# Six sums of weights moved from block 1 to behind batch 0's rows, and a multiplication by g moved from block 2's second group to its third

## The chip, the cores and the metric

The kernel runs on one core of a Trainium2 chip. The metric is the time of one execution in device microseconds (us), as the median of several runs. A profiled execution gives the trace: its span is the time from the first to the last instruction, and its own time has a little more around it. The engines are TensorE (PE), VectorE (DVE), ScalarE (ACT), GpSimd (POOL) and SyncE (SP), each with a queue of its own that it works through in order. PEld is TensorE's load of weights, beside its products.

## The reference

Eight batches of eight heads, 576 tokens, 64 values a head. Attention without a softmax, a normalization with a gain g, and then a gated layer with GELU and a gated residual:

```python
kv = np.einsum('bhsd,bhse->bhde', k, v)
out = np.einsum('bhsd,bhde->bhse', q, kv)
rms = np.sqrt(np.mean(out * out, axis=-1, keepdims=True) + 1e-06)
x = out / rms * g_norm          # then (4608, 512), heads side by side
g = x @ w_gate                  # (4608, 1536)
gelu = 0.5 * g * (1.0 + erf(g * inv_sqrt2))
ffn_out = gelu * (x @ w_val) @ w_out
res_gate = 1.0 / (1.0 + np.exp(-(x @ w_res)))
result = x + res_gate * ffn_out
```

## The kernel before

The rows are worked in nine blocks. Blocks 0 to 7 hold the first 512 tokens of each batch, as four groups of 128 rows (`NJ = 4`); block 8 holds what remains of all eight batches. While a block is in the gated layer, the attention of a later batch is computed in between.

A block's first half multiplies its transposed rows, `xT_t[blk]`, by the weights of the gate and of the value, 12 tiles of 128 columns (`NF = 12`). Block 1 takes the tiles one by one (`m_gval`, lines 434 for TensorE, 422 for ScalarE's GELU, 423 for VectorE's product `hid`). From block 2 on, the columns come in three groups of four tiles (`gv_group`). A group computes its 2 by 2 blocks of products with seven products instead of eight, with sums of weights and sums of rows made beforehand. The weight sums are `wsg` and `wsv` (`weight_sums`, one `tensor_tensor` of VectorE at line 503 for each part; all of the kernel's `sub` calls have this line). The token sums are `ts` (`token_sums`). One set of weight sums is made for each group and each of gate and value: four sums a set. For group 0, whose columns lie in two tiles of weights, each sum takes two instructions of 128x256. Block 0 uses the seven products for its last group alone, so the sums of group 0 are wanted first by block 2.

The order of words within a group is a string, `ORDERS`. A digit with g or v is a product on TensorE (four matmuls, line 971); E and d are ScalarE's copies; F and c are VectorE's sums (line 992); g11 to g22 are GELUs; h11 to h22 are the products `hid` (line 1008; h22 on GpSimd, the others on VectorE). For the last group it is

```python
True: "1g 1v Eg 5g Ev 5v dg 6g dv 6v Fg 2g Fv 2v 7g g11 7v cg 3g cv 3v h11 g22 4g g12 h12 4v g21 h22 h21",
```

Product 7 adds to the bank that F has read, so 7g waits for Fg, and 7v for Fv.

The second half of a block (`out_by_products`, lines 540 and 503) multiplies `hid` by the output weights, again with seven products: wA, wD, wE and wF are TensorE's banks. Its last product, on wA, waits for VectorE's subtraction `osb` at line 503, which reads the bank first. Block 0 does this half plainly, with 48 matmuls (`out_by_f`, fps at line 472).

Attention of a batch b: `a_qT` or a transposing transfer gives qT, `a_kv` the 64x64 products, `a_o` the outputs `op`; ScalarE squares them (`a_sq`, line 263), VectorE reduces the squares (`a_red`, line 268, `ss`), `a_norm` makes the inverse root (on VectorE for batches 1 and 2, on GpSimd later), `a_t` writes the rows t (line 368), and a transpose, on TensorE for batch 1 (`a_xT`, xtp, line 375) and by a transfer later (`d_xT`), gives xT. The gain g enters xT by `a_g`, one `tensor_scalar` of VectorE at line 394 for two groups of rows; the rows t themselves, which the residual needs, are multiplied by g in `row_times_g` (line 385): for batch 0 on VectorE (`a_x`), for later blocks on GpSimd.

What sets the order: the program is written out by hand. Each block has numbered slots. `at(blk, slot, ...)` puts work behind a slot, `aside_out(blk, word, ...)` at a named point of the second half ("D", "F", "00", "22", "01", "11", "end"), and `at_word(blk, group, word, ...)` behind a word of a group. Each instruction goes to its engine's queue in the order in which the program reaches it. In block 0, slot 15 (`NF + 3`) is the point behind the fourth product of the residual gate; `plan_attn_1` puts batch 1's qT, the loads of batch 2 (GpSimd's queue) and batch 0's rows there. The reductions of batch 1 come next on VectorE, from `amid_step[3, 1]`. In block 1, slot 2 comes early in the gate and value products, slots 10 and 11 at their end.

`plan_attn_ahead(b)` spreads the attention of batch b over block m = b - 2 and the next. For b = 3, block m + 1 is block 2, the first that is `whole` (all three groups by seven products): `first_whole`.

Of the kernel before, what the change touches and what calls it, by code (L numbers as in the profile page):

```python
# [18 lines left out]
def kernel(  # L19
# [115 lines left out]
    def by_token(b, copy=nc.vector.tensor_copy, js=slice(0, NJ)):  # L135
        copy(
            out=b16_t[b, "q"].rearrange("p j h d -> p h j d")[:, :, js, :],
            in_=raw[b, "q"].rearrange("p h (j d) -> p h j d", j=NJ)[:, :, js, :],
        )
# [39 lines left out]
    def attn_begin(b):  # L179
        st[b] = {  # L180
            "qT": attnp.tile([P, NJ, NP, P], FP16, tag="qT", bufs=1, name="qT"),
            "kv2": (
                attnp.tile([P, NP, D], FP16, tag="kv2", bufs=4, name="kv2")
                if b > 0
                else t_t[B][:, NJ - 1, :].rearrange("p (r c) -> p r c", r=NP)
            ),
            "ss": attnp.tile([P, NJ + 1, H], FP32, tag="ss", name="ss"),
            "o": {},
        }

    def a_qT(b, jj):

        q16 = b16_t[b, "q"].rearrange("p j h d -> p j (h d)")
        ps = pattn.tile([P, 2, NP, P], FP16, tag="at", name="qtp")
        for e in range(2):
            for pr in range(NP):
                nc.tensor.transpose(ps[:, e, pr, :], q16[:, 2 * jj + e, pr * P : (pr + 1) * P], ident)
        nc.scalar.copy(out=st[b]["qT"][:, 2 * jj : 2 * jj + 2, :, :], in_=ps)
# [71 lines left out]
    def a_ss(b, i):  # L270
        a_sq(b, i)
        a_red(b, i)
# [81 lines left out]
    def where(b, j):  # L354
        return (b, j) if j < NJ else (B, pair(b))

    def a_t(b, i):

        o, rinv = st[b]["o"][i], st[b]["rinv"]
        if i < NJ:  # L360
            jj, e = i // 2, i % 2
            t = t_t[b][:, 2 * jj : 2 * jj + 2, :].rearrange("p j (r e d) -> p j r e d", e=2, d=D)[:, :, :, e, :]
            scale = of_o(rinv, i)[:, :, :, None].to_broadcast([P, 2, NP, D])
        else:
            t = t_t[B][:, pair(b), :].rearrange("p (h d) -> p h d", h=H)
            o = o.rearrange("p (h d) -> p h d", h=H)
            scale = rinv[:, NJ, :, None].to_broadcast([P, H, D])
        nc.vector.tensor_tensor(out=t, in0=o, in1=scale, op=ALU.mult)  # L368

    def a_xT(b, j, eng=nc.scalar):  # L370

        blk, jj = where(b, j)
        ps = pattn.tile([P, NP, P], FP16, tag="at", name="xtp")
        for cc in range(NP):
            nc.tensor.transpose(ps[:, cc, :], t_t[blk][:, jj, cc * P : (cc + 1) * P], ident)
        if eng is nc.scalar:
            nc.scalar.activation(out=xT_t[blk][:, jj, :, :], in_=ps, func=AF.Copy, scale=gcol)
        else:
            eng.tensor_scalar(out=xT_t[blk][:, jj, :, :], in0=ps, scalar1=gcol, scalar2=None, op0=ALU.mult)

    def a_x(b, j, eng=nc.vector):
        row_times_g(*where(b, j), eng)

    def row_times_g(blk, jj, eng):
        eng.tensor_tensor(out=t_t[blk][:, jj, :], in0=t_t[blk][:, jj, :], in1=g16, op=ALU.mult)  # L385

    def a_g(b, j0, j1, eng=nc.vector):

        blk, k0 = where(b, j0)
        xs = xT_t[blk][:, k0 : k0 + j1 - j0, :, :]  # L390
        if eng is nc.scalar:
            nc.scalar.activation(out=xs, in_=xs, func=AF.Copy, scale=gcol)
        else:
            eng.tensor_scalar(out=xs, in0=xs, scalar1=gcol, scalar2=None, op0=ALU.mult)
# [955 lines left out]
    def attn_plan_1():  # L1350

        b = 1
        ss = [lambda j=j: a_ss(b, j) for j in range(NJ)]
        t = [lambda j=j: a_t(b, j) for j in range(NJ)]
        x = [lambda j=j: a_xT(b, j) for j in range(NJ)]
        plan = {
            NF - 1: [lambda: by_token(b)],
            NF + 3: [
                lambda: attn_begin(b),
                lambda: a_qT(b, 0),  # L1360
                lambda: a_qT(b, 1),
                lambda: load_batch(b + 1),
                *[lambda j=j: a_x(0, j) for j in range(NJ)],
            ],
            NF + 6: [lambda: a_kv(b, nc.scalar.copy)],
            NF + 8: [lambda: a_norm(b, 0, NJ), *t],
            2 * NF + 2: [x[0]],
        }
        amid_step[3, 1] = [lambda: a_o(b), *ss]
        amid_step[NF - 1, 1] = [x[1], lambda: a_xT(b, 2, nc.vector)]  # L1370
        amid_step[NF - 1, 3] = [x[3]]
        return plan
# [13 lines left out]
    def at(blk, slot, *fs):  # L1386
        plans[blk].setdefault(slot, []).extend(fs)

    def aside_out(blk, ahead_of, *fs):
        amid_out.setdefault(blk, {}).setdefault(ahead_of, []).extend(fs)  # L1390
# [32 lines left out]
    def plan_attn_ahead(b):  # L1423

        rem = pair(b) is not None
        m = b - 2
        assert rem == (m in GROUPS)
        act, pool = nc.scalar.copy, nc.gpsimd
        begin = [lambda: attn_begin(b), lambda: d_qT(b)]
        if rem:  # L1430
            at_word(m, 0, "h22", begin.pop(0), lambda: d_rem_qT(b))
        if m in GROUPS:
            for i in range(2):
                half = lambda i=i: by_token(b, act, slice(2 * i, 2 * i + 2))
                if whole(m):
                    at_word(m, i, "g11", half)
                else:
                    at(m, 2 + i, half)
            if whole(m):
                at_word(m, 1, "g11", *begin)  # L1440
            else:
                at(m, 3, *begin)
            if b + 1 < B:
                at(m, 2 * GF, lambda: load_behind(b))
            last = len(GROUPS[m]) - 1
        else:
            at(m, 8, lambda: by_token(b, act, slice(0, 2)))
            at(m, 9, lambda: by_token(b, act, slice(2, 4)), *begin)
            at(m, NF, lambda: a_kv(b, act), lambda: load_behind(b, load_q))
            aside_out(m, "end", lambda: load_kv(b + 1))  # L1450
        if rem:
            at_word(m + 2, 0, "cv", lambda: a_g(b, NJ, NJ + 1))
            own = 2 * pair(b) + 1 == b
            at_word(m, last, "5v" if own else "3g", lambda: a_rem_kv(b))
            at_word(m, last, "dv" if own else "g12", lambda: kv_out(b))
            if own:
                at_word(m, last, "3g", lambda: rem_mm(b))
            at_word(m, last, "g12", lambda: rem_out(b))
        else:
            at(m, NF + 1, lambda: a_o(b), lambda: a_ss(b, 0), lambda: a_ss(b, 1))  # L1460
            aside_out(m, "D", lambda: a_ss(b, 2), lambda: a_ss(b, 3))
        aside_out(m, "F", lambda: a_norm(b, 0, NJ + rem, pool))
        first = [lambda: new_block(b), lambda: a_t(b, 0), lambda: a_t(b, 1)]
        if whole(m + 1):
            aside_out(m, "01" if m + 1 == WHOLE else "11", *first[0:2])
            upper = [] if m + 1 == WHOLE else [lambda: d_xT(b, 0, 2)]
            amid_out[m].setdefault("end", [])[0:0] = [first[2], *upper]
        else:
            at(m, NF + 3, *first)
        if whole(m + 1):  # L1470
            t = [lambda j=j: a_t(b, j) for j in range(NJ)]
            if rem:
                at_word(m + 1, 0, "h21", lambda: a_t(b, NJ), lambda: d_xT(b, NJ, NJ + 1))
            first_whole = m + 1 == WHOLE
            for i, word, fs in (
                (0, "Fv", t[2:3]),
                (0, "cv", [t[3], lambda: d_xT(b, 0 if first_whole else 2, NJ)]),
                (1, "h21" if first_whole else "cv", [lambda: a_g(b, 0, 2)]),
                (2, "Fv", [lambda: a_g(b, 2, NJ)]),
            ):  # L1480
                at_word(m + 1, i, word, *fs)
            return
        for j in range(2, NJ + rem):
            at(m + 1, j - 2, lambda j=j: a_t(b, j))
        at(m + 1, 1, lambda: d_xT(b, 0, NJ))
        at_word(m + 1, 1, "Fv", lambda: a_g(b, 0, 2))
        at_word(m + 1, 1, "cv", lambda: a_g(b, 2, NJ))
# [6 lines left out]
    at(0, 7, *sums["v", 2][0:2])  # L1494
    at_word(0, 0, "1v", *sums["v", 2][2:4])
    late_sums = [f for u in (("g", 0), ("v", 0)) for f in sums[u]]
    for i, f in enumerate(late_sums[0:6]):
        at(1, (2, 10, 11)[i // 2], f)
    aside_out(1, "22", *late_sums[6:8])
    for blk in GROUPS:  # L1500
        t = token_sums(blk, nc.vector)
        if blk == 2:
# [169 lines left out]
```

## Time and profile before

| | us |
|---|---|
| median of 3 runs (320.03 to 321.11) | 320.2 |
| profiled execution | 321.38 |
| its span | 319.6 |
| blocks 0 and 1's start: VectorE busy, 37.3 to 55.0 | 14.27 of 17.70 |
| block 1's first half: VectorE busy, 55.0 to 77.3 | 20.48 of 22.30 |
| block 1's second half: VectorE busy, 77.3 to 91.7 | 13.57 of 14.40 |
| block 2's three groups: VectorE busy, 91.7 to 112.0 | 19.25 of 20.30 |

The stages are windows of the trace, in us from the span's start. The mean granted clock of TensorE is 0.99. The page's slices of the span, in tenths of each fortieth, show how the engines are filled:

```profile
PE   7899999999999999999999999999999999999993
PEld 2655755544788888888888888888888888888882
DVE  5797968989899999989998999899988777897774
ACT  4673665566838794878587858695767467836760
POOL 2874260450599578857885788517861375396332
```

A matmul's end in the trace is modelled, and each overlaps the next, so TensorE's pace is read from the distance of starts. VectorE too starts an instruction a little before the last one has ended. A bracket behind a line gives the idle time ahead of it and what ended that.

### The profile page before, as it was taken

How to read it: one execution, taken by the hardware profiler on the slowest of the kernel's cores; microseconds unless marked ns; L12 is line 12 of the kernel's file. 1: busy time of each engine (PE TensorE's matmuls, PEld its weight loads, DVE VectorE, ACT ScalarE, POOL GpSimd, SP SyncE). 2: the span in 40 equal slices, each digit the busy share in tenths (PEclk: the TensorE clock that was granted, in tenths of full speed). 3: DMA queues.
4: the chain of work that ended last, by engine and by line, in shares of the span. 5: the costliest groups of instructions: out<-in, count | busy, mean ns of one | idle time of the engine just before them, and what ended most of it. 6: DMA issues, size and time to landing. Idle time of an engine off the chain costs nothing.

```text
span 319.6 us, 7776 instructions
## 1 busy us (share of the span) xinstructions
PE 310.7 (97%) x3047; PEld 247.6 (77%) x3047; DVE 277.2 (87%) x493; ACT 209.9 (66%) x385; POOL 185.3 (58%) x238
## 2 busy tenths in 40 slices
PE   7899999999999999999999999999999999999993
PEld 2655755544788888888888888888888888888882
DVE  5797968989899999989998999899988777897774
ACT  4673665566838794878587858695767467836760
POOL 2874260450599578857885788517861375396332
PEclk9799999999999999999999999999999999999998
DMA  7999999999939899379967993800440003001204
GB/s 251 327 169 205 201 197 199 188 140 204 134 37 195 199 131 115 72 215 113 120 84 215 99 135 74 219 10 0 68 148 2 2 2 133 0 2 49 85 2 131
DMA packets 77398, 38.91 MB, mean 122 GB/s; under 512 B 42290, under 2 KB 75058, under 8 KB 77362
## 3 DMA queue, kind: packets, MB, share of 16 engines
q0 software_dynamic: 39296, 17.17, 43.6%
q1 hardware_dynamic: 37488, 20.71, 25.0%
q8 instruction: 24, 0.39, 0.5%
q10 hardware_dynamic: 578, 0.52, 0.5%
q14 instruction: 12, 0.10, 0.1%
HBM read 38.80 MB, written 9.44 MB: 151 GB/s over the span
## 4 chain that ended last, share of the span: by engine, by line
PE 92%; DVE 4%; DMA 2%; SPq 1%; issue 1%; ACT 0%; DVEq 0%
PE Av L971 12%; PE Ag L971 12%; PE wA L540 12%; PE Fv L971 6%; PE Fg L971 6%; PE gps L434 5%; PE vps L434 5%; PE rA L591 4%; PE Ev L971 3%; PE wD L540 3%; PE Eg L971 3%; PE wE L540 3%; PE w L540 2%; PE wF L540 2%; PE rps L455 2%; PE rF L591 2%
## 5 line engine op out<-in xcount | busy, mean ns | idle before, releaser
L1008 POOL TENSOR_TENSOR hid<-ge,c 128x512 f16<-128x512 f16 x22 | 25.8, 1174 | 36.6 <-ACT ge L1002 36.6
L540 PEld LDWEIGHTS <-hid_s 128*128 128x128 f16 x384 | 37.5, 98 | 4.4
L385 POOL TENSOR_TENSOR t<-t,g 128x512 f16<-128x512 f16 x32 | 37.8, 1210 | 0.0
L971 PEld LDWEIGHTS <-wsg 128*128 128x128 f16 x352 | 34.3, 98 | 4.4 <-issue 0.3
L971 PEld LDWEIGHTS <-wsv 128*128 128x128 f16 x352 | 34.0, 98 | 4.8 <-issue 0.4
L727 POOL TENSOR_TENSOR osb<-osb,t 128x512 f32<-128x512 f32 x28 | 34.0, 1244 | 0.0
L981 ACT COPY Eg<-Ag 128x512 f32<-128x512 f32 x22 | 12.8, 583 | 28.0 <-PE Ag L971 28.0
L540 PEld LDWEIGHTS <-hid 128*128 128x128 f16 x288 | 28.1, 98 | 3.6 <-issue 0.3
L971 PEld LDWEIGHTS <-wg 128*128 128x128 f16 x264 | 25.8, 98 | 3.2
L971 PEld LDWEIGHTS <-wv 128*128 128x128 f16 x264 | 25.8, 98 | 3.0
L971 PE MATMUL Ag<-ts,wsg 128*128 128x256 f16 x176 | 26.4, 273 | 0.2 <-DVE Fg L992 0.2
L971 PE MATMUL Av<-ts,wsv 128*128 128x256 f16 x176 | 26.4, 272 | 0.0
L992 DVE TENSOR_TENSOR Fg<-Ag,d 128x512 f32<-128x512 f32 x22 | 15.3, 695 | 10.3 <-ACT d L985 6.4
L268 DVE TENSOR_REDUCE ss<-sq 128x8 f32<-128x512 f32 x32 | 20.5, 679 | 3.2 <-ACT sq L263 3.2
L422 ACT ACTIVATE ge<-gps 128x512 f16<-128x512 f32 x20 | 11.8, 597 | 14.3 <-PE gps L434 13.5
L540 PE MATMUL wA<-wo_ts,hid_s 128*128 128x256 f16 x168 | 20.6, 273 | 0.0
L1002 ACT ACTIVATE ge<-Eg 128x512 f16<-128x512 f32 x22 | 13.1, 597 | 9.7 <-PE Eg L971 9.7
L1002 ACT ACTIVATE ge<-c 128x512 f16<-128x512 f32 x22 | 13.8, 625 | 8.5 <-DVE c L992 8.5
L368 DVE TENSOR_TENSOR t<-op,ny 128x512 f16<-128x512 f32 x28 | 18.7, 684 | 0.5
L434 PE MATMUL gps<-xT,wg 128*128 128x512 f16 (+1 forms) x76 | 18.7, 368 | 0.0
L434 PE MATMUL vps<-xT,wv 128*128 128x512 f16 (+1 forms) x76 | 18.7, 368 | 0.0
L1002 ACT ACTIVATE ge<-Fg 128x512 f16<-128x512 f32 x22 | 13.0, 590 | 8.5 <-PE Fg L971 6.5
(224 smaller groups left out, 856.2 us busy)
## 6 DMA issues: line engine op xcount, KB each, us to landing
out_dram<-osb SPq DMA_DIRECT2D x14, 512.0 KB, 3.5
qraw<-in_q_dram POOLq DMA_DIRECT2D x7, 512.0 KB, 7.2
k<-in_k_dram POOLq DMA_DIRECT2D x7, 512.0 KB, 8.5
v<-in_v_dram POOLq DMA_DIRECT2D x7, 512.0 KB, 10.3
wo<-in_moe_w_out_dram POOLq DMA_DIRECT2D x3, 384.0 KB, 11.7
wg<-in_moe_w_gate_dram POOLq DMA_DIRECT2D x2, 512.0 KB, 9.2
out_dram<-osb SPq DMA_DIRECT2D x4, 256.0 KB, 4.4
wv<-in_moe_w_val_dram POOLq DMA_DIRECT2D x3, 256.0 KB, 8.3
```

The costliest lines, as they stand in the source:

```text
L268: nc.vector.tensor_reduce(out=out_, in_=sqs.pop((b, i)), op=ALU.add, axis=mybir.AxisListType.X)
L368: nc.vector.tensor_tensor(out=t, in0=o, in1=scale, op=ALU.mult)
L385: eng.tensor_tensor(out=t_t[blk][:, jj, :], in0=t_t[blk][:, jj, :], in1=g16, op=ALU.mult)
L434: nc.tensor.matmul(ps[:, j0 * P : j1 * P], lhsT=w[:, cc, :], rhs=xT_t[blk][:, j0:j1, cc, :], start=(cc == 0 and j0 == 0), stop=(cc == NP - ...
L540: nc.tensor.matmul(ps[:, e - es[0], :], lhsT=a[:, f, e * P : (e + 1) * P], rhs=b[:, f, :], start=(start and e == es[0] and f == 0), stop=( ...
L591: nc.tensor.matmul(out_[:, e, :], lhsT=x_[:, e, cc, :], rhs=w_[:, cc, :], start=(first and e == 0 and cc == 0), stop=(cc == 1), skip_group ...
L727: nc.gpsimd.tensor_tensor(out=res_all[of], in0=res_all[of], in1=t_t[blk][of], op=ALU.add)
L971: nc.tensor.matmul(out_[:, r, :], lhsT=lhsT, rhs=rhs, start=(first and r == 0 and c == 0), stop=(c == 1), skip_group_check=True,)
L981: nc.scalar.copy(out=tile_of("E", u), in_=ps["A", u])
L992: nc.vector.tensor_tensor(out=dst, in0=ps["A", u], in1=sb["d", u], op=ALU.add)
L1002: nc.scalar.activation(out=ge[q], in_=source(q, "g"), func=AF.Gelu)
L1008: eng.tensor_tensor(out=dst, in0=ge[q], in1=source(q, "v"), op=ALU.mult)
```

## The change

```diff
@@ attn_plan_1, block 0 @@
                 lambda: load_batch(b + 1),
                 *[lambda j=j: a_x(0, j) for j in range(NJ)],
+                *late_sums[0:6],
             ],
@@ plan_attn_ahead @@
                 (0, "Fv", t[2:3]),
                 (0, "cv", [t[3], lambda: d_xT(b, 0 if first_whole else 2, NJ)]),
-                (1, "h21" if first_whole else "cv", [lambda: a_g(b, 0, 2)]),
+                (2 if first_whole else 1, "Fv" if first_whole else "cv", [lambda: a_g(b, 0, 2)]),
                 (2, "Fv", [lambda: a_g(b, 2, NJ)]),
@@ the weight sums @@
     late_sums = [f for u in (("g", 0), ("v", 0)) for f in sums[u]]
-    for i, f in enumerate(late_sums[0:6]):
-        at(1, (2, 10, 11)[i // 2], f)
-    aside_out(1, "22", *late_sums[6:8])
+    at(1, 2, *late_sums[6:8])
```

`late_sums` are the eight sums of group 0, gate first. Before, two of them stood in each of block 1's slots 2, 10 and 11, and two at "22" of its second half, ahead of the subtraction `osb`. Now the first six stand in block 0's slot 15, behind batch 0's rows, and the last two in block 1's slot 2, the third. In block 2, `a_g(3, 0, 2)`, for the first two groups of batch 3's rows, stood behind the last word of group 1; now it stands behind Fv of group 2, directly ahead of `a_g(3, 2, 4)`. For other batches `a_g` stays. What is computed is the same.

## The prediction

> **What bounds the kernel now.** I read the page's busy times first, then the chain of work that ended last, then the timelines of TensorE, VectorE and GpSimd around the places that the diff touches.
>
> ```profile
> PE 310.7 (97%) x3047; PEld 247.6 (77%) x3047; DVE 277.2 (87%) x493; ACT 209.9 (66%) x385; POOL 185.3 (58%) x238
> ```
>
> TensorE (PE) is busy for 97% of the span, so the kernel ends earlier only where a stall of TensorE goes away, and later only where one is made. VectorE (DVE) comes next; what it does behind TensorE costs nothing. The chain of waits shows where VectorE stands in TensorE's way:
>
> ```profile
> 46.19 0.59 ACT sq L263
> 46.78 0.02 issue
> 46.81 2.48 DVE ss L268 x4
> ...
> 51.39 2.50 DVE t L368 x4
> 53.89 0.05 issue
> 53.93 0.40 PE xtp L375 x4
> ...
> 89.12 0.54 DVE wsv L503 x2
> 89.66 0.61 DVE osb L503
> 90.27 0.04 issue
> 90.31 1.47 PE wA L540 x12
> ...
> 106.69 0.25 issue
> 106.94 0.70 DVE Fg L992
> 107.64 0.04 issue
> 107.68 0.60 PE Ag L971 x4
> ```
>
> There are three such places. From 46.81 to 53.93, at the end of block 0, the chain runs through VectorE's work for batch 1: a delay there reaches TensorE one for one. At 89.12 two weight sums stand ahead of the subtraction (osb, L503) that the last product of block 1 waits for. At 106.94 Fg is late. TensorE's timeline gives the sizes (columns: start, length, instructions):
>
> ```profile
> 88.70 1.47 PE L540 MATMUL wF<-wo,hid_s 128*128 128x256 f16 x12
> 90.31 1.47 PE L540 MATMUL wA<-wo_ts,hid 128*128 128x256 f16 x12
> 106.91 0.60 PE L971 MATMUL Ev<-xT,wv 128*128 128x256 f16 x4
> 107.68 0.60 PE L971 MATMUL Ag<-ts,wsg 128*128 128x256 f16 x4 [0.17 <-DVE Fg L992]
> 108.28 0.60 PE L971 MATMUL Av<-ts,wsv 128*128 128x256 f16 x4
> ```
>
> Twelve products normally follow one another at 1.31 us (87.39 to 88.70); here wA comes 1.61 behind wF: 0.30 lost. Four products normally take 0.44; Ag comes 0.77 behind Ev and Av 0.60 behind Ag: 0.33 + 0.16 = 0.49 lost. After 124 us TensorE's timeline shows no idle stretch up to the tail. VectorE's timeline shows the causes, and the gap that the change fills:
>
> ```profile
> 42.93 1.43 DVE L385 TENSOR_TENSOR t<-t,g 128x512 f16<-128x512 f16 x4
> 46.81 0.69 DVE L268 TENSOR_REDUCE ss<-sq 128x8 f32<-128x512 f32 x1 [2.45 <-ACT sq L263]
> 61.69 0.49 DVE L503 TENSOR_TENSOR wsg<-wg 128x256 f16<-128x256 f16 x2
> 62.10 0.49 DVE L503 TENSOR_TENSOR wsg<-wsg,wg 128x256 f16<-128x256 f16 x2
> 62.50 0.42 DVE L229 CAST kv<-kvp 128x256 f16<-128x256 f32 x1
> 104.87 2.15 DVE L394 TENSOR_SCALAR xT<-xT,gcol 128x1024 f16<-128x1024 f16 x1
> ```
>
> Behind batch 0's rows (t times g) VectorE is idle for 2.45 us until ScalarE's squares arrive. A weight sum is two instructions that take 0.405 us in the queue (61.69 to 62.10). And the multiplication by g at 104.87 took 2.15 us where its like takes 0.48 (140.71, block 3).
>
> **What the Trainium skill says.** "SBUF — State Buffer", section "SBUF: two separate sides", says that VectorE and GpSimd share a pair of ports as an exclusive lock held for a whole instruction: a VectorE instruction in a two-port mode takes it against any GpSimd work, one with two SBUF inputs only against GpSimd work that reads SBUF. "VectorE: DVE Perf Modes", "Why tensor_tensor can't do 2×_2P or 4×", says the sums can't be in such a two-port mode, since the second port carries the second tensor; the g multiplication has one tensor and can. The trace agrees on both: GpSimd's product of 105.58 (1.15 us) lies inside the 2.15 us of the g multiplication, and a 128x512 sum at 39.66 took 1.89 us beside GpSimd's product at 40.08, against 0.42 elsewhere. The same SBUF section warns that a two-port instruction keeps GpSimd from writing the descriptors of the transfers it issues. By the page that does not hold for the sums; in the trace, the sums of 23.89 and 25.30 stand beside the issues of wo (23.70, 0.75 us) and v (25.07, 0.92 us), and both sides keep their usual lengths.
>
> **The change part by part.** The instruction lists of the two kernels differ on VectorE alone; the order on TensorE, ScalarE, GpSimd and SP is the same, so no transfer is moved past anything.
>
> Part 1, six sums to block 0. Twelve 128x256 instructions come behind the rows and ahead of the first reduction (ss). 6 x 0.405 = 2.43 us. An instruction starts some 0.08 before its forerunner's end (61.09 + 0.68 = 61.77, next at 61.69), so they start at 44.36 - 0.08 = 44.28 and free the queue at 46.71. The reduction can't start before 46.81, since the squares end at 46.78. Cover 2.45 us, cost 2.43: nothing on the path, with 0.1 us in hand. Their inputs are long there: TensorE itself multiplied by these columns before 25 us (gps and vps of the first four column tiles). What waits behind them is the reduction, and then the normalization, the rows t, and TensorE's transposes at 53.93. Two bounds for the cost: nothing below, as the squares set the start; above, at the slower pace of 0.45 per pair that the sums show at 88.67 to 89.58 beside GpSimd's small operations, 6 x 0.45 = 2.70, the queue is free at 46.98 and the path loses 0.17. During the gap GpSimd only issues transfers (k 44.15, v 45.01, and the two small ones to 47.26), beside which sums kept their pace, so I take nothing.
>
> If instead GpSimd's issues were held by the sums, batch 2's last piece, which lands at 46.6 + 12.6 = 59.2 and is wanted by TensorE at 60.25, has 1.1 us in hand. Transfer engines are saturated there, so a later issue need not mean a later landing.
>
> Part 2, the sums leave block 1. Slot 2 keeps four instructions (the last two sums in place of the first two): no change. At slots 10 and 11 eight leave, 4 x 0.405 = 1.6 us; VectorE meets ScalarE's squares at 82.79 anyway with 0.50 idle, and TensorE shows no gap there: nothing gained. Ahead of osb four leave, 0.90 us. Then osb starts when the product wA is done: 88.86 plus the 0.12 that the like subtraction at 86.36 stood behind its product, 88.98 instead of 89.58. From its start to TensorE's last product were 0.73 us (89.58 to 90.31), so that one could start at 89.71, and TensorE reaches it at 90.01: 0.30 gained whole. Next, VectorE's row t at 90.84 waits for GpSimd's normalization (to 90.80), which doesn't move, so VectorE may enter block 2 no earlier than now. Fg of 93.92 to 94.62 is wanted at 94.82 (95.12 less 0.30), and Fv, to 95.21, at 95.26: just in time; should that slip, I put 0.1 to it. Bounds 0.20 and 0.30; I take 0.30.
>
> Part 3, g. In block 2 the first of batch 3's two g multiplications leaves the end of group 1 and stands in front of the second one, behind Fg and Fv of group 2. Then Fg waits for its product (105.60 + 0.60 = 106.20) and ScalarE's copy d (to 106.22): 106.25 instead of 106.94. It ends at 106.95, and Ag can follow Ev at 107.35. Fv takes 106.85 to 107.54, ahead of Av at 107.79. That returns the 0.49. The nearest rows bound it: in block 3, where no g stands ahead of Fg, Fg still started late (139.50) and Ev to Fg of TensorE took 1.53 (139.76 to 141.29) for 1.31: 0.22 lost; in block 4 (172.40 to 173.71) 1.31, nothing lost. So 0.27 to 0.49; I take 0.40. The two g multiplications cost 2 x 0.39 in the queue (86.96 to 87.87, two of them). They lie at 107.45 to 108.24 in today's times, where GpSimd is idle until 109.95 and so can't block them. c, behind them, comes no later than today (108.53). xT of batch 3 isn't wanted before the token sums at 121.01.
>
> Sum: 0 + 0.30 + 0.40 = 0.70 us of TensorE's stalls. The profiled execution, 319.6 of span and 321.38 in all, becomes 318.9 and 320.7. The median of the runs, 320.2, is 1.2 below that execution, though their work is the same; the difference goes onto the median: 319.5. Change and run-to-run scatter are close: 0.3%, about what a measurement of this kernel can tell from no change, is 0.96 us, and the gain is 0.22%.
>
> **The rivals.**
> - Everything returned and a little more: 0.30 + 0.49 = 0.79 and some 0.2 from VectorE being freer in blocks 1 and 2, where I see TensorE without gaps. For it: GpSimd's normalization would run without sums beside it and end sooner. Against it: TensorE has nothing more to give there. 319.2 or less.
> - Only one of the two stalls goes, because the row t behind the normalization, or the wait seen in block 3, is late next. For it: block 3's 139.50. Against: block 4. A gain of 0.30: 319.9.
> - Slower: in the gap of block 0, GpSimd's four issues and the sums exclude each other, although rows of 23 to 26 us say otherwise. The issues last 3.1 us (44.15 to 47.26); all of that in series gives a reduction 3.1 later, and 3.1 - 0.70 = 2.4 us more: 322.6; half of it 321.0. This decides once a sum's instruction takes over 0.26 us ((2.45 + 0.70) / 12); slower by 0.3% from (2.45 + 0.70 + 0.96) / 12 = 0.34. For it: the same kind of instruction took 1.89 us beside GpSimd's product, and the gap has 0.1 us to spare.
>
> **How the numbers follow.** Forecast 0.47, everything and more 0.25, one stall only 0.11, slower 0.17. The likeliest gives 319.5. The range goes down to 318.8, for the fuller gain, and up to 320.9, for the single stall and an overrun of 0.17 to 1.4 us in block 0; most of the slower rival's chance and the edge of the fuller gain stay out. Faster by over 0.3%: 0.28 (the fuller gain, and the edge of the forecast). Slower by over 0.3%: 0.16. Within: 0.56.
>
> **What would show it.** Part 1 is right if ss of block 0 starts at 46.8 with hardly any idle time before it and the transposes at 53.9 stay; wrong if sums there last over 0.3 us each. Part 2 is right if wA follows wF at 1.31 at the end of block 1. Part 3 is right if Ev, Ag and Av of block 2's last group come 0.44 apart and both g multiplications take under 0.5. The prediction fails if the reduction of block 0 moves by over 0.3 us, or if a transfer (the kvp products at 60.25) becomes a wait.

## The result, and the profile after

| | before | after |
|---|---|---|
| median (range), 22 runs each | 320.5 us (319.94 to 322.15) | 319.89 us (319.19 to 320.72) |
| profiled execution | 321.38 | 319.31 |
| its span | 319.6 | 317.5 |

The ratio of after to before is 0.9977, with a 95% interval of 0.9966 to 0.9988. The gain is 0.23% or 0.74 us (0.38 to 1.09); it is below 0.3%, but over so many runs it can be told from no change. Single executions of some kernels below ran over 2% longer at a lower granted clock; medians and ratios are given without them.

The page of after gives the busy times

```profile
PE 308.5 (97%) x3047; PEld 246.6 (78%) x3047; DVE 275.7 (87%) x493; ACT 209.5 (66%) x385; POOL 185.5 (58%) x238
```

TensorE is busy for the same 97% and the instruction counts are those of before: work was moved, none was saved. The two spans differ by 2.1 us, and most of that isn't the change. In the windows of the trace for 5.00 to 20.80 us (columns: the stretch, its length, busy time of PE, PEld, DVE, ACT and POOL with instruction counts, TensorE's granted clock, DMA share, GB/s), the kernel before shows

```profile
5.00:20.80 15.80, 13.99 (x108) 8.60 (x107) 11.88 (x32) 11.33 (x23) 12.44 (x18) 0.89 1.14 281
```

and the kernel after

```profile
5.00:20.80 15.80, 13.53 (x114) 8.04 (x113) 12.77 (x35) 11.94 (x25) 13.01 (x19) 1.00 1.19 292
```

The clock was 0.89 in one and 1.00 in the other, ahead of anything that the diff touches, and block 0's residual gate (rps) starts 1.24 us earlier in the profile after. The change has to be read from the distances behind that point:

| start of a TensorE group | before | after | earlier by |
|---|---|---|---|
| rps, block 0 | 37.16 | 35.92 | 1.24 |
| third gate product of block 1 | 56.63 | 55.33 | 1.30 |
| wF, end of block 1 | 88.70 | 87.40 | 1.30 |
| last wA of block 1 | 90.31 | 88.71 | 1.60 |
| Ev, last group of block 2 | 106.91 | 105.35 | 1.56 |
| Ag | 107.68 | 105.78 | 1.90 |
| Fg | 108.71 | 106.66 | 2.05 |
| last product | 312.60 | 310.56 | 2.04 |

It gives 0.30 at the end of block 1, takes 0.04 at the start of block 2, and gives 0.49 in block 2's last group: 0.75 us, all of it still there at the end. The runs' ratio gives 0.74. The step from 1.24 to 1.30 isn't the change's: it comes ahead of the two fps products at 45.21 (43.90 in after), which wait for none of the moved sums.

TensorE's timeline of after at the two places (start, length, instructions):

```profile
87.40 1.47 PE L540 MATMUL wF<-wo,hid_s 128*128 128x256 f16 x12
88.71 1.47 PE L540 MATMUL wA<-wo_ts,hid 128*128 128x256 f16 x12
...
105.35 0.60 PE L971 MATMUL Ev<-xT,wv 128*128 128x256 f16 x4
105.78 0.60 PE L971 MATMUL Ag<-ts,wsg 128*128 128x256 f16 x4
106.22 0.60 PE L971 MATMUL Av<-ts,wsv 128*128 128x256 f16 x4
106.66 0.60 PE L971 MATMUL Fg<-xT,wsg 128*128 128x256 f16 x4
```

wA follows wF at 1.31 us, and the four groups follow one another at 0.43 to 0.44: both stalls are gone. VectorE's timeline of after shows the moved work:

```profile
41.70 1.43 DVE L385 TENSOR_TENSOR t<-t,g 128x512 f16<-128x512 f16 x4
43.04 0.49 DVE L503 TENSOR_TENSOR wsg<-wg 128x256 f16<-128x256 f16 x2
...
45.06 0.49 DVE L503 TENSOR_TENSOR wsv<-wsv,wv 128x256 f16<-128x256 f16 x2
45.50 2.46 DVE L268 TENSOR_REDUCE ss<-sq 128x8 f32<-128x512 f32 x4
...
87.65 0.69 DVE L503 TENSOR_TENSOR osb<-wA,wd 128x512 f32<-128x512 f32 x1 [0.21 <-PE wA L540]
...
104.75 0.70 DVE L992 TENSOR_TENSOR Fg<-Ag,d 128x512 f32<-128x512 f32 x1 [1.36 <-ACT d L985]
...
105.95 0.88 DVE L394 TENSOR_SCALAR xT<-xT,gcol 128x1024 f16<-128x1024 f16 x2
```

The six sums fill 43.04 to 45.55, and the reductions start right behind them: of the 2.45 us of idle time nothing is left, and no bracket stands behind ss. At the end of block 1, osb waits for its product wA now, and no longer for sums. In block 2, Fg waits for ScalarE's d only, and the two multiplications by g take 0.88 us together. The page's chain of waits puts the sums on the path itself (start, length, what):

```profile
41.79 1.34 DVE t L385 x4
43.13 1.62 DVE wsg L503 x8
44.75 0.81 DVE wsv L503 x4
45.56 2.42 DVE ss L268 x4
```

ScalarE's squares begin at 44.87 in this profile and the first of them is done about 0.60 later (one square's time in all_eight's trace), at 45.47. The reductions start 0.03 behind that, as they did before (46.78 and 46.81). The sums cost nothing there, but only just: they and the squares end together.

### The profile page after: what moved, and what is told of

Its sections match the earlier page's. It is cut to its first block, busy times and chain, and to the rows that moved or that the text cites. A ratio compares the mean times of both kernels' runs of the same rounds, so it can differ in the third digit from the quotient of the medians.

```text
span 317.5 us, 7776 instructions
## 1 busy us (share of the span) xinstructions
PE 308.5 (97%) x3047; PEld 246.6 (78%) x3047; DVE 275.7 (87%) x493; ACT 209.5 (66%) x385; POOL 185.5 (58%) x238
## 3 DMA queue, kind: packets, MB, share of 16 engines
q0 software_dynamic: 39296, 17.17, 43.2%
## 4 chain that ended last, share of the span: by engine, by line
PE 81%; DVE 6%; issue 0%; DVEq 0%
PE Av L971 12%; PE Ag L971 12%; PE wA L540 12%; PE Fv L971 6%; PE Fg L971 6%; PE rA L591 4%; PE gps L434 3%; PE vps L434 3%; PE Eg L971 3%; PE wF L540 3%; PE wE L540 3%; PE wD L540 3%; PE Ev L971 3%; PE w L540 2%; PE rF L591 2%; PE kvp L218 1%
```

## The experiments

In all of them "the ratio" is that of the kernel to the kernel before on the same chip, with a 95% interval, and TensorE's distances are between starts.

### Each part alone

The first kernel (sums_alone) is after with g back in its old place; the second (g_alone) is before with g moved.

```diff
@@ sums_alone, against after @@
-                (2 if first_whole else 1, "Fv" if first_whole else "cv", [lambda: a_g(b, 0, 2)]),
+                (1, "h21" if first_whole else "cv", [lambda: a_g(b, 0, 2)]),
@@ g_alone, against before @@
-                (1, "h21" if first_whole else "cv", [lambda: a_g(b, 0, 2)]),
+                (2 if first_whole else 1, "Fv" if first_whole else "cv", [lambda: a_g(b, 0, 2)]),
```

> The sums moved as in the change, g left where it was. Theory (the two stalls are separate): block 1's last product follows wF at 1.31 us instead of 1.61, and in block 2's last group Ev, Ag, Av stay at 0.77 and 0.60; 0.30 us of TensorE's time gained, some 0.1% of the kernel. Rival (the 0.30 only frees VectorE, and the change's gain is all in g): the last product still comes at 1.6, nothing gained. Slower rival: the reduction ss of block 0 starts later than 0.1 us behind the squares.

> g moved as in the change, the sums left where they were. Theory: Ev, Ag, Av of block 2's last group come 0.44 apart, 0.49 us gained, 0.15%; block 1's last product stays at 1.61. Rival (one stall hides behind the other, since VectorE enters block 2 late because of the sums): under 0.3 gained here, and the two single runs do not add to the change's 0.79.

Measured: sums_alone 320.3 us, ratio 0.9986 (0.9976 to 0.9997); g_alone 320.2 us, ratio 0.9983 (0.9969 to 0.9998).

| | wF to wA | Ev to Ag, Ag to Av |
|---|---|---|
| before | 1.61 | 0.77, 0.60 |
| sums_alone | 1.31 | 0.78, 0.59 |
| g_alone | 1.62 | 0.44, 0.44 |
| after | 1.31 | 0.43, 0.44 |

Each part removes its own stall and leaves the other's alone. The local sizes, 0.30 and 0.49, lie within what the ratios say (0.1 to 0.8 us and 0.1 to 1.0 us); the ratios alone are too coarse to tell 0.30 from 0.49.

### What the six sums cost, and how much more the gap holds

all_eight puts the last two sums behind the rows as well, where the cover is used up.

```diff
-                *late_sums[0:6],
+                *late_sums,
             ],
...
-    at(1, 2, *late_sums[6:8])
```

> The change, with all eight sums behind batch 0's rows: sixteen instructions, 3.24 us, in a gap of 2.45. Theory (the gap is filled to within 0.1 us and the chain behind it reaches TensorE one for one): the reduction ss starts 0.73 later than ScalarE's squares allow, the transposes xtp wait 0.7 longer, and the time is 0.7 us above the change, level with the kernel before. Rival (VectorE's work there has room): under 0.2 us above the change.

Measured: 320.27 us, ratio 0.9992 (0.998 to 1.0005). The distance that holds the whole seam, from the pair of fps products ahead of batch 1's outputs to block 1's third gate product, comes out as follows. TensorE's timeline of after:

```profile
43.90 0.59 PE L472 MATMUL fps<-wo,hid 128*128 128x512 f16 x2
...
55.33 1.03 PE L434 MATMUL gps<-xT,wg 128*128 128x512 f16 x4
```

and of all_eight:

```profile
44.87 0.61 PE L472 MATMUL fps<-wo,hid 128*128 128x512 f16 x2
...
56.68 1.03 PE L434 MATMUL gps<-xT,wg 128*128 128x512 f16 x4
```

| sums in the gap | kernels | distance, us |
|---|---|---|
| none | before, g_alone | 11.42, 11.43 |
| six | after, sums_alone | 11.43, 11.42 |
| eight | all_eight | 11.81 |

Six sums cost 0.01 us at most, in every profile. Two more cost 0.39, where 0.7 was expected: in that profile the squares were done at 45.85 + 0.60 = 46.45 and the reductions came at 46.86, 0.41 late, as VectorE's timeline of all_eight shows:

```profile
43.63 0.49 DVE L503 TENSOR_TENSOR wsg<-wg 128x256 f16<-128x256 f16 x2
...
46.45 0.49 DVE L503 TENSOR_TENSOR wsv<-wv,wsv 128x256 f16<-128x256 f16 x2
46.86 2.46 DVE L268 TENSOR_REDUCE ss<-sq 128x8 f32<-128x512 f32 x4
```

What VectorE is late there reaches TensorE one for one (0.41 and 0.39). Two sums take 0.81, so six would have had 0.4 us in hand there, while in after's profile they had none. The room isn't fixed. From rps on, the sums start 0.13 us earlier in all_eight than in after, and the squares 0.26 later. The later squares come from TensorE, whose products kvp waited longer for batch 1's vl to land, from the first at 43.67 on (its timeline, with the idle time and its reason in the bracket):

```profile
44.24 0.22 PE L218 MATMUL kvp<-vl,kl 128*64 128x64 f16 x2 [0.25 <-DMA vl<-in_v_dram]
```

The slower rival wanted GpSimd's issues of transfers and the sums to exclude each other. GpSimd's timeline of after, beside the sums of 43.04 to 45.55:

```profile
42.82 0.87 POOL L130 DMA_DIRECT2D k<-in_k_dram  x1 [1.65 <-issue]
```

The issue of v follows at 43.69. Before, the same two stood 0.86 us apart (44.15 and 45.01) beside an idle VectorE, and the sums keep their 0.40 to 0.41 a pair. Neither side held the other. The Trainium skill says so of such instructions ("SBUF — State Buffer", section "Who interferes with whom": a `tensor_tensor` takes the shared pair's read interface alone, and writing descriptors needs the write interface), and marks it as inferred; here it is measured for two-input sums of 128x256.

### Could the two sums have stayed near block 1's end

sums_slot11 is before with the last two sums moved only a little: from the point ahead of osb to slot 11, the end of the first half.

```diff
-    aside_out(1, "22", *late_sums[6:8])
+    at(1, 11, *late_sums[6:8])
```

> The kernel before, with only the last two sums moved, from in front of the subtraction to block 1's slot 11; nothing goes to block 0. Theory (only the two sums ahead of the subtraction cost time, and VectorE has 0.5 us idle behind slot 11): block 1's last product follows wF at 1.31, 0.30 gained as by the whole move; the reduction of the squares behind slot 11 starts some 0.3 later, which its wait for TensorE covers. Rival (block 1's end is too full, so the move to block 0 is needed): wD, wA or wE comes later, or the last product stays over 1.5.

This kernel ran once, in 328.51 us, and TensorE's clock fell to 0.6 in one late slice of it; so only its trace up to block 2 is used. TensorE's timeline there:

```profile
87.29 1.47 PE L540 MATMUL wF<-wo,hid_s 128*128 128x256 f16 x12
88.61 1.47 PE L540 MATMUL wA<-wo_ts,hid 128*128 128x256 f16 x12
...
90.79 0.60 PE L971 MATMUL Fg<-ts,wsg 128*128 128x256 f16 x4
91.50 0.60 PE L971 MATMUL Ag<-ts,wsg 128*128 128x256 f16 x4
92.04 0.60 PE L971 MATMUL Fv<-ts,wsv 128*128 128x256 f16 x4
```

wA follows wF at 1.32: the 0.30 is there. But Ag follows Fg at 0.71 and Fv follows at 0.54, where 0.44 each is normal: 0.27 + 0.10 = 0.37 is lost at once. The chain of waits of the same kernel says on what:

```profile
89.22 0.27 POOL ny L334
89.48 0.02 issue
89.50 0.69 DVE t L368
90.20 0.60 DVE osb L723
...
90.88 0.58 ACT Eg L981
91.46 0.04 issue
91.50 0.60 PE Ag L971 x4
```

Two sums more at slot 11 make the reductions later (the first starts 5.70 us ahead of wF, for 5.91 before), and with them GpSimd's normalization (ny); VectorE's row t waits for it, osb (the step that reads wF's bank) waits behind t, and ScalarE's copy Eg of block 2 is behind that. So the cost of a place in block 1 isn't at the place.

In after the reductions start as before (5.92 us ahead of wF), although four sums have left slots 10 and 11. What changes is the length of the normalization. GpSimd's timeline of before, beside the sums of 88.67 to 89.66:

```profile
88.93 0.38 POOL L328 TENSOR_TENSOR na<-na,nm 128x32 f32<-128x32 f32 x1
89.40 0.34 POOL L330 TENSOR_SCALAR nh<-na 128x32 f32<-128x32 f32 x1
```

and the same two operations in after, with no sums beside them (why the sums make them longer the traces don't say):

```profile
87.62 0.25 POOL L328 TENSOR_TENSOR na<-na,nm 128x32 f32<-128x32 f32 x1
87.96 0.22 POOL L330 TENSOR_SCALAR nh<-na 128x32 f32<-128x32 f32 x1
```

From its first operation (nm) to its last (ny) the normalization takes 4.58 to 4.59 us in the four kernels with sums ahead of osb (before, before_h22, g_alone, h22_vector) and 4.32 to 4.34 in the eight without (after and all made from it). So the row t starts 1.88 us behind wF in after, for 2.14 before and 2.21 in sums_slot11. From 1.88 to 2.21 the loss at block 2's start grows from 0.04 to 0.37; so at 2.14 it would be some 0.30 (an estimate from these figures), as much as the move gains at wA. The gain stays because the sums no longer run beside the normalization either. Whether the four sums of slots 10 and 11 had to leave block 1 was not tried; the unchanged start of the reductions speaks against it.

### What made the multiplication by g take 2.15 us

h22_vector is before, with GpSimd's one product of block 2's group 1 (h22) on VectorE and g in its old place. If it is that product which holds g's ports, the stall must go without moving g.

```diff
-            eng = nc.gpsimd if q == "22" else nc.vector
+            eng = nc.gpsimd if q == "22" and (blk, g) != (2, 1) else nc.vector
```

> The kernel before, with one product (h22 of block 2's second group) on VectorE, behind g, instead of GpSimd. Theory (the g multiplication waits for GpSimd: first for its addition, which ends at 105.6, and then for this product, which takes the ports first): g takes 0.8 to 1.2 us instead of 2.15; with 0.6 for the product on VectorE, Fg comes 0.3 to 0.8 earlier than before. Rival (g waits for the transposed rows or is slow for another reason): g still takes about 2.1.

One run, 319.97 us. VectorE's timeline:

```profile
104.14 1.03 DVE L394 TENSOR_SCALAR xT<-xT,gcol 128x1024 f16<-128x1024 f16 x1
...
105.70 0.68 DVE L992 TENSOR_TENSOR Fg<-Ag,d 128x512 f32<-128x512 f32 x1
```

GpSimd's:

```profile
100.40 4.49 POOL L727 TENSOR_TENSOR osb<-osb,t 128x512 f32<-128x512 f32 x4
```

The multiplication takes 1.03 us instead of 2.15, and Ev, Ag and Av come 0.43 and 0.44 apart: the stall is gone, although VectorE has one product more. GpSimd's last addition ends at 104.89, and the multiplication 0.28 behind it. Before, it ended 0.29 behind GpSimd's product (107.02 and 106.73). That the product held it is shown by the run without it; that it waited for the addition too, and that the shared ports are what it waited for, is inferred from these times.

### Two edits beyond the change

x2_late is after, with the transposes of batch 1's last rows two products later in block 0's list, so that TensorE does products and not a wait. h22_first is after, with block 0's h22 on VectorE: near 38 us GpSimd's product of block 0 falls on VectorE's instructions.

```diff
@@ x2_late, against after @@
-        amid_step[NF - 1, 1] = [x[1], lambda: a_xT(b, 2, nc.vector)]
-        amid_step[NF - 1, 3] = [x[3]]
+        amid_step[NF - 1, 1] = [x[1]]
+        amid_step[NF - 1, 3] = [lambda: a_xT(b, 2, nc.vector), x[3]]
@@ h22_first, against after @@
-            eng = nc.gpsimd if q == "22" else nc.vector
+            eng = nc.gpsimd if q == "22" and blk > 0 else nc.vector
```

> The change, and batch 1's third transpose behind two more of block 0's last products instead of ahead of them. Theory (TensorE stands 0.28 us in front of the third transpose, waiting for the rows t): the wait is covered by the two products, 0.2 to 0.28 us gained over the change. Rival (the wait moves to block 1's first products, which need these rows' copies): nothing gained, as the copies come later by the same time.

> The change, with h22 of block 0's group on VectorE instead of GpSimd. In some profiles the copy of q for batch 1 (L136) takes 2.1 to 2.4 us beside this product, in others a weight sum takes 1.9; where it is the copy, TensorE's transposes qtp start 0.6 to 0.85 us later. Theory (the collision is a lottery that costs TensorE in part of the runs): no instruction of VectorE there takes over 0.7, the distance from the first rps to the first fps is 4.35 in every profile, the runs scatter less, and the median is 0.2 to 0.5 below the change. Rival (the product only changes engines, and VectorE is as late by it): no difference, or 0.2 slower.

x2_late: 319.47 us, ratio 0.9966 (0.9953 to 0.9979). The seam (fps pair to third gate product) takes 55.51 - 44.34 = 11.17 us for the 11.43 of after: 0.26 gained. Its trace is also without a loss of 0.22 us in block 3, as are those of three kernels that leave the transposes alone (see part 3 below).

h22_first: 319.15 us, ratio 0.9965 (0.9952 to 0.9978). What it avoids shows best in g_alone, whose VectorE has

```profile
37.80 2.35 DVE L136 COPY q<-qraw 128x2048 f16<-128x2048 f16 x1
```

and whose TensorE has

```profile
40.21 1.07 PE L197 MATMUL qtp<-ident,q 128*128 128x128 f16 x16 [0.68 <-DVE q L136]
```

while h22_first has, on VectorE,

```profile
38.39 0.68 DVE L136 COPY q<-qraw 128x2048 f16<-128x2048 f16 x1
```

In g_alone the copy of q lay beside GpSimd's product (38.42, 1.17 us), and TensorE's transposes waited for it: rps to fps took 5.20 us, against 4.35 in h22_first. In x2_late it was 2.11 and 4.97. In the profiles of before and after it was the next instruction, a weight sum (1.89 and 1.90 us), for which nobody waits: 4.50 and 4.35 (where the 0.15 more of before comes from is not shown). In after_again and all_eight it was the sum behind that one (1.76 and 1.77 us). From rps to the two fps products ahead of batch 1's outputs, TensorE takes 8.40 and 8.64 us where q is hit, 7.90 to 8.23 in the seven profiles where a sum is, and 7.78 to 7.91 in the four with h22 on VectorE. So the edit earns 0.5 to 0.9 us where q is hit and at most 0.45 where a sum is. h22_first's trace is also without block 3's 0.22. Its runs don't scatter less, as had been expected: 318.89 to 321.74 us.

Two more kernels ask whether that gain needs the change, and whether the edits add up: before_h22 is before with h22_first's edit, and both is after with the two edits. They ran beside a second run of after.

> The kernel before, with only h22 of block 0's group on VectorE instead of GpSimd. Theory (the collision at 38 to 41 us belongs to the kernel before too and has nothing to do with the change): 0.3 to 0.7 us under the kernel before, rps to fps 4.35, block 1's last product still at 1.61 and block 2's Ev, Ag, Av still at 0.77 and 0.60. Rival (the gain of the run with h22 on VectorE came from the room that the moved sums had lost there): no difference from the kernel before.

> The change, with the third transpose late and h22 of block 0 on VectorE. Theory (the two gains are separate): 0.28 us below the run with h22 alone, 0.5 to 0.8 below the change. Rival (VectorE's chain behind the rows is late again): no better than the run with the late transpose.

> The changed kernel, beside the next two on one chip. Theory: 0.7 to 0.8 us under the kernel before; in its profile, the distance from the first rps to the first fps is either 4.35 or 5.0 to 5.2, as a weight sum or the copy of q meets GpSimd's product. Rival (the distance is fixed by the program): 4.35 again and no spread.

> The change with both further edits, beside the change on one chip. Theory: 0.5 to 0.9 us under the change and 1.2 to 1.6 under the kernel before. Rival (the two edits' gains do not add, as block 3's late Fg of 0.22 comes back): 0.5 or less under the change.

| kernel | runs | median, us | ratio to before |
|---|---|---|---|
| both (chip of h22_first) | 14 | 319.1 | 0.995 (0.9932 to 0.9968) |
| after_again | 21 | 319.82 | 0.9976 (0.9968 to 0.9985) |
| before_h22 | 8 | 319.75 | 0.9973 (0.9956 to 0.9989) |
| both_again (chip of the two above) | 9 | 319.07 | 0.9964 (0.9948 to 0.9979) |

The change's gain comes back: 0.9976 after 0.9977. In after_again's profile rps to fps takes 4.35 us again, so no spread within one kernel is shown; the copy of q was hit in one profile each of g_alone and x2_late.

before_h22 keeps both of the change's stalls (wF to wA 1.61; Ev to Ag to Av 0.78 and 0.59) and is yet 0.27% faster than before, 0.87 us (0.35 to 1.41). So this gain doesn't need the change. The traces show some 0.5 us of it: 0.27 from rps to the fps pair (8.05 and 7.78 us) and 0.22 in block 3. Only the first can be the collision near 38 us.

both gains 0.5% on the kernel before by the first of its two ratios and 0.36% by the second. It is 0.75 us below after's second run by the medians and some 0.4 by the ratios, whose intervals overlap; that doesn't decide between the 0.5 to 0.9 expected and the rival's 0.5 or less. Nor is both measurably below h22_first (319.1 and 319.15 us on one chip), where 0.28 was expected. The traces say why: the seam is 0.26 shorter (11.15 us for 11.41), but in block 3 Ev to Fg takes 1.54 us in both and 1.31 in h22_first. The 0.22 comes back, as the rival of both_again had it.

## Why the prediction was right, point by point

The forecast was a gain of 0.70 us; the traces show 0.75 and the ratio 0.74 (0.38 to 1.09). What it said of each part's stall and its removal held. Two steps inside did not: that GpSimd's normalization doesn't move (part 2), and the discount for block 3 (part 3). The absolute 319.5 was 0.4 too low, 0.3 of it because it was counted from 320.2, the median of three runs; the same kernel's median over 22 is 320.5. The span of 318.9 forecast for the profile came out at 317.5, for the most part by the clock in the opening.

- **Part 1, taken at nothing.** Right: the seam takes 11.42 and 11.43 us without the sums and 11.43 and 11.42 with them. The 2.43 us worked out for them was 2.42 to 2.46. The 0.1 us in hand was the uncertain term: there was nothing in after's profile, and about 0.4 in all_eight's. all_eight showed that what goes beyond the cover reaches TensorE one for one. The slower pace of 0.45 per pair didn't come up.
- **Part 2, taken at 0.30.** Measured 0.30 in after and in sums_alone. The 0.1 set aside for a late Fg wasn't needed: product 7 follows Ev at 0.44 (93.12 to 93.56). The 0.04 lost at block 2's start stands four products earlier (Ag to Fv 0.48, 91.33 to 91.81). That slots 10 and 11 give nothing by themselves is in line with 32.07 us from the third gate product to wF in both kernels. One step failed: the prediction took GpSimd's normalization as fixed and still expected to keep the 0.30. By the estimate from sums_slot11's figures an unmoved normalization would have cost about that much. It ended 0.26 us sooner, which the prediction had named only under its rival with the fuller gain. That the 0.30 was kept is luck in this step.
- **Part 3, taken at 0.40.** The term was mis-sized: 0.49, its upper bound, in after and in g_alone. The discount came from block 3's 0.22 us (a loss that the prediction's "no idle stretch" after 124 us passes over). In after, block 2 doesn't have that loss, and block 3 has it as before (its Ev to Fg takes 1.54). It is another kind of wait, as VectorE's timeline shows, in after and then in before_h22:

```profile
137.45 0.70 DVE L992 TENSOR_TENSOR Fg<-Ag,d 128x512 f32<-128x512 f32 x1 [0.93 <-PE Av L971]
...
137.66 0.70 DVE L992 TENSOR_TENSOR Fg<-Ag,d 128x512 f32<-128x512 f32 x1 [0.60 <-ACT d L985]
```

In after, Fg's inputs are there at 137.09 (d), and it starts 0.36 later, behind the product Av (to 137.43), which it doesn't read. In before_h22 it starts 0.04 behind d. All nine profiles with the loss show the wait for Av, and the four without it (x2_late, h22_first, before_h22, h22_vector) the wait for d; a kernel profiled twice shows the same both times. So the loss belongs to the kernel and not to VectorE being late. Why Fg waits for Av in some kernels stays open.
- **The rival with a fuller gain** was given for VectorE being freer elsewhere. Its sign came, since the normalization ends sooner, but that only kept the 0.30; nothing more is gained, and from Fg of block 2 to the end the distance is the same to 0.01. **Only one stall goes** fell in both parts. **The slower rival** fell: the sums took 0.20 us each and not 0.26, and GpSimd's issues kept their length.

## What to carry to other kernels

Work that stands ahead of a late instruction was free here where it was moved into a wait whose end another engine sets, and that wait's room differed by 0.4 us between two profiles; so compare the work with the shortest wait that several profiles show. When two engines share ports, look at what the *other* engine does and has next in its queue: moving one instruction of either away from the meeting point in block 2 gave back the whole 0.49 us. The two engines also slowed each other where the trace shows no wait: without the two sums beside it, GpSimd's normalization was 0.26 us shorter. Compare two kernels from a landmark behind their common opening, not by their spans: here 1.3 of 2.1 us had nothing to do with the change. And compare them part by part: a loss of 0.22 us in block 3 comes and goes with edits that don't touch it.

## What the runs showed of the hardware that was not expected

- **A waiting VectorE instruction wasn't next in line.** By its times the multiplication by g waited for GpSimd's addition, and then GpSimd's product went ahead of it too: 2.15 us, against 1.03 with the product gone and 0.44 in its new place. The Trainium skill's "SBUF — State Buffer", "Who interferes with whom", says that the first to issue holds the pair for a whole instruction; who is next it leaves open.
- **The instruction hit near 38 us isn't always the one that is running.** In after the sum started at 38.42 and would have ended at 38.84; GpSimd's product started at 38.85, and the sum lasted until 40.32. In before it was 39.66, 40.08 and 41.55. In five of the nine profiles with such a hit, the instruction hit was still in its usual time when the product started; in four (before, after, sums_alone, h22_vector) that time had just run out, by up to 0.16 us. By the recorded starts VectorE's instruction was first each time, and it yet ended behind the product, a sum by about 0.3 us and the copy of q by 0.55. No run here tells why.
- **The wait for batch 1's vl differs from profile to profile.** In after TensorE reaches batch 1's products at 42.95, and their second group comes at 43.25, 0.30 later, where before it was 0.19: vl, issued at 27.62, lands 15.6 us later, at 43.2. So TensorE waited 0.1 us there in after, and in all_eight, where the second group comes 0.60 later, 0.4. Whether this is why the medians of versions that differ in block 0 lie closer together than their stalls was not tried.
